# The last output stores of a linear-attention and MLP block: one block half stored by SyncE alone, ScalarE's last stores ordered behind two of SyncE's

## The chip, the cores and the metric

The kernel runs on one core of a Trainium2 chip. The metric is the device time of one execution in microseconds: the median of the runs, 405.24 us for the kernel before. A core has TensorE (PE in the profile), VectorE (DVE), ScalarE (ACT), GpSimd (POOL) and SyncE (SP). SP, ACT and POOL can each issue DMAs, and those of one issuer wait in its own queue; 16 DMA engines move the data.

## The reference

```python
xn = _layernorm(x)                                   # x: 2048 tokens x 512
qkv = xn @ wqkv                                      # 32 heads of 16
pq, pk = phi(q), phi(k)                              # phi(t) = where(t>0, t+1, exp(t)) + 1e-6
kv = einsum("bhsd,bhse->bhde", pk, v);  z = sum_s pk
o = (pq @ kv) / (pq . z + 1e-6)
h = xn @ w1 + b1;  h = relu(h) ** 2                  # 1376 hidden units
return x + o @ wo + (h @ w2 + b2)
```

The output is 2048 x 512 in float32. Only its last stores are touched by the change.

## The kernel before

Tokens are worked on in four blocks of 512. A first part normalises all of them, forms the keys' sums and prepares the weights; then a loop `for n in range(2)` produces the output, two blocks per turn: `t1, t2 = NB - 1 - 2 * n, NB - 2 - 2 * n`. Products of 2x2 blocks are made with Strassen-like combinations (seven products instead of eight), every float32 operand being split into a high and a low part (`split`: ACT rounds the high part, DVE subtracts to get the low one, both in a tile `s`), and three matmul passes are made of the two. At the end of the second turn (n = 1, blocks t1 = 1 and t2 = 0) the partial sums are added up by phases: `phase_jobs(X, 6)`, `phase_jobs(Y, 3)`, `phase_jobs(X, 7)`. What `at_end(...)` names runs after a phase's last job.

An output block is collected in a tile `res[t]` of 128 partitions x 2 halves x 16 x 64. It starts out as x; `add_turned(res[t], c, src)` transposes a result 32 by 32 on DVE (tile `o`) and adds it in. A half (columns 0 to 255 or 256 to 511 of the output) is complete when two such adds are done. In the profile `res[t1]` is res_3127 and `res[t2]` is res_3212.

`store(r, t, *halves, by, blocks)` (line 1315) writes a half with four DMAs, one for each group g = 0, 32, 64, 96 of 32 partitions, each 128 KB in runs of 64 floats. SP issues them; where `by` names another engine, that one issues the groups 32 and 96 (`g.start % 64`) and SP the groups 0 and 64.

Four block halves are stored at the end of the second turn:

- t2's half 1, after phase 6 (line 1633): SP for g = 0 and 64, ACT for g = 32 and 96;
- t1's half 0 (early ready) and half 1, after phase 3 (line 1635): half 0 by SP, half 1 by SP for g = 0 and 64 and by POOL for g = 32 and 96;
- t2's half 0, after the last phase, in two parts of eight 32-token rows each (`PARTS`, `flush`, line 1640): per part SP stores g = 0 and 64, ACT stores g = 32 and 96, 64 KB each. These eight stores of 64 KB are the last work of the program.

What sets the order: the code only records instructions. `Program.order` plans them with costs per instruction, a queue per engine, and dependencies by region of a tile (a write after a read of the same bytes depends on it; writes to the output tensor are not compared). TensorE's own order is fixed as recorded. The instructions are then emitted in the planned order, line 328, which is why nearly all rows of the profile name that line.

A second thing hangs on the emitted order. Every DMA that SP or ACT issues gets one of eight completion semaphores, DMAHW0 to DMAHW7, in turn, over both engines together; before it is issued, the issuing engine waits until the DMA that had the same semaphore eight places earlier has landed. POOL's DMAs have semaphores of their own.

Of the kernel before, what the change touches and what calls it, by code (L numbers as in the profile page):

```python
# [339 lines left out]
def kernel(  # L340
# [12 lines left out]
    nc = Program(tc.nc)  # L353
# [57 lines left out]
    def w512(name, tag, bufs):  # L411
        return work.tile([P, 512], F32, name=name, tag=tag, bufs=bufs)
# [11 lines left out]
    def four(name, tag, dt=F32, pool=None):  # L424
        return (pool or work).tile([P, TB, 512], dt, name=name, tag=tag)
# [13 lines left out]
    def copy(eng, o, i, bias=0.0):  # L439
        if eng == "act":  # L440
            nc.scalar.activation(o, i, AF.Copy, bias=bias)
        elif bias:
            ENG[eng].tensor_scalar(o, i, bias, None, op0=OP.add)
        else:
            ENG[eng].tensor_copy(o, i)
# [600 lines left out]
    for i0 in range(0, NT, TB):  # L1046
# [4 lines left out]
        else:  # L1051
            o = four(f"xg{i0}", "r0" if i0 + TB == NT else "r3")
            a, o = (t.rearrange("p a (g c) -> p (a g c)", g=NJ) for t in (a, o))
            groups[i0 + TB - 1] = [t.rearrange("p (g n) -> p g n", g=NJ) for t in (a, o)]
            a, o = (t.rearrange("p (g i c) -> p g i c", g=NJ, i=TB) for t in (a, o))
# [240 lines left out]
    def out_blocks(w, t):  # L1296

        rows = w[t * BT:(t + 1) * BT, :].rearrange("(b t) n -> t b n", t=32)
        return [(slice(32 * g, 32 * (g + 1)), h, rows[:, :, 256 * h + 64 * g:256 * h + 64 * (g + 1)])
                for h in range(2) for g in range(NJ)]  # L1300

    def load_res(t, pool, tag):
        r = pool.tile([P, 2, BT // 32, 64], F32, name=f"res{t}", tag=tag)
        for g, h, rows in out_blocks(xf, t):
            nc.sync.dma_start(r[g, h], rows)
        return r

    def add_turned(r, c, src, part=slice(0, BT)):
        blocks = slice(part.start // 32, part.stop // 32)
        o = w512("o", "d", 2)[:, :part.stop - part.start]  # L1310
        nc.vector.transpose(o, src[:, part])
        at = r[:, c // 2, blocks].rearrange("p b (d c) -> p b c d", c=2)[:, :, c % 2]
        nc.vector.tensor_tensor(out=at, in0=o.rearrange("p (b d) -> p b d", d=32), in1=at, op=OP.add)

    def store(r, t, *halves, by=None, blocks=slice(0, BT // 32)):
        for g, h, rows in out_blocks(of, t):
            if h in halves:
                (by or nc.sync if g.start % 64 else nc.sync).dma_start(rows[:, blocks], r[g, h, blocks])
# [10 lines left out]
    for n in range(2):  # L1329
        t1, t2 = NB - 1 - 2 * n, NB - 2 - 2 * n  # L1330
# [87 lines left out]
        for p in range(NK + 1):  # L1418
# [20 lines left out]
            if f_before:  # L1439
# [6 lines left out]
                elif p == NK:  # L1446
                    b = [bank(f"late{k}", loop_tag) for k in range(TB)]
                    X, V, Z, Y = b[1:3], [b[3], b[0]], acc[:2], acc[2:]
# [38 lines left out]
        o, ends, res = {}, {}, {}  # L1487
# [7 lines left out]
        def add_to(o, ps):  # L1495
            for c in range(2):
                nc.vector.tensor_tensor(out=o[c], in0=ps[c], in1=o[c], op=OP.add)

        def turned_to(t, a, src):
            for c in range(2):  # L1500
                add_turned(res[t], a + c, src[c])

        def at_end(f):
            ends.setdefault(len(jobs) - 1, []).append(f)
# [94 lines left out]
        X, Z = acc[:2], acc[2:]  # L1599
        res = {t1: load_res(t1, keep, "B0"), t2: load_res(t2, keep, "A0")}  # L1600
# [12 lines left out]
        def phase_jobs(ps, i, first=False, last=False):  # L1613
            return [strassen(ps, k, i, first and k == pairs_f[0], last and k == pairs_f[-1]) for k in pairs_f]
# [15 lines left out]
        jobs.append((lambda: hz[:, 1], lambda s: second_z(W, range(2, NJ), s, True, True)))  # L1630
        at_end(lambda: add_to(o["m5"], W))
        jobs += phase_jobs(X, 6)
        at_end(lambda: (add_to(o["m5"], X), turned_to(t2, 2, o["m5"]), store(res[t2], t2, 1, by=nc.scalar)))
        jobs += phase_jobs(Y, 3, False, True)
        at_end(lambda: (add_to(o["u2"], Y), turned_to(t1, 2, o["u2"]), store(res[t1], t1, 0), store(res[t1], t1, 1, by=nc.gpsimd)))
        jobs.append((lambda: hz[:, 1], lambda s: second_z(X, range(2), s)))
# [2 lines left out]

        def flush(part):  # L1640
            add_turned(res[t2], 1, ends_in[part.start], part)
            store(res[t2], t2, 0, by=nc.scalar, blocks=slice(part.start // 32, part.stop // 32))

        at_end(lambda: run(lambda: add_turned(res[t2], 0, X[0]), *[lambda part=part: flush(part) for part in PARTS]))

        def prepare_s(job):
# [33 lines left out]
```

## Time and profile before

| what | us |
|---|---|
| median of 3 runs (405.2 to 405.49) | 405.24 |
| the profiled execution's own time | 405.01 |
| its span, first to last instruction | 403.3 |
| PE busy | 395.9 (98%) |
| DVE busy | 345.2 (86%) |
| ACT busy | 273.7 (68%) |
| POOL busy | 52.3 (13%) |
| granted TensorE clock | 0.999 |

How to read it: PE is busy nearly throughout, so little but its own work can move the time while it runs. Behind PE's last matmul only DVE's last adds, the eight last stores and the program's end remain; this tail has to be read from the rows of the last microseconds, since shares of the span do not show it. DMA-issuing instructions are listed as `SPq`, `ACTq` and `POOL` rows: their duration is the time that the issuer spends on the issue, not the transfer's.

### The profile page before, as it was taken

The numbers are of one execution on the slowest core, as the hardware profiler recorded it, in microseconds if no ns is written. First come the engines' busy times: TensorE is split into PE (matmuls) and PEld (weight loads), VectorE is DVE, ScalarE is ACT, GpSimd is POOL, SyncE is SP. The second block draws the span as 40 slices with busy tenths as digits, with TensorE's granted clock in tenths as the row PEclk, the third lists the DMA queues.
The fourth block names the chain that finished last, engine by engine and source line by source line (L and its number), as shares of the span: only waits on it lengthen the run. The fifth ranks groups of instructions, "written<-read, shape, count | busy, mean of one in ns | idle before, by whom it ended". The sixth has DMA issues, their size and how long they took to land.

```text
span 403.3 us, 5554 instructions
## 1 busy us (share of the span) xinstructions
PE 395.9 (98%) x1781; PEld 328.3 (81%) x1781; DVE 345.2 (86%) x556; ACT 273.7 (68%) x467; POOL 52.3 (13%) x68
## 2 busy tenths in 40 slices
PE   8999999999999999999999999999999999999994
PEld 7788888888888888888888888888888888888883
DVE  5898998989578989999998899947999999886784
ACT  5786666765859999879986632476968877455430
POOL 2242422120221121220000000031011100000001
PEclk9999999999999999999999999999999999999999
DMA  7962625712398679698627999988998769999345
GB/s 231 292 189 72 201 61 143 295 52 105 122 320 307 232 254 329 242 351 292 265 90 212 325 251 321 287 239 274 301 301 313 243 200 266 234 273 292 111 132 105
DMA packets 77841, 92.00 MB, mean 228 GB/s; under 512 B 39122, under 2 KB 50386, under 8 KB 77556
## 3 DMA queue, kind: packets, MB, share of 16 engines
q1 hardware_dynamic: 75572, 90.86, 73.6%
q10 hardware_dynamic: 2144, 0.52, 0.6%
q0 software_dynamic: 96, 0.26, 0.3%
q8 instruction: 14, 0.23, 0.2%
q14 instruction: 15, 0.12, 0.1%
HBM read 54.67 MB, written 34.87 MB: 222 GB/s over the span
## 4 chain that ended last, share of the span: by engine, by line
PE 96%; DVE 2%; DMA 1%; issue 0%
PE ps L328 54%; PE acc L328 42%; DMA x<-in_A_x_dram 1%; DVE res L328 0%; DVE o L328 0%; DVE st L328 0%; DVE xp L328 0%; DVE y L328 0%; DVE mv L328 0%
## 5 line engine op out<-in xcount | busy, mean ns | idle before, releaser
L328 PE MATMUL ps<-s,ops 128*128 128x512 f32 x417 | 97.9, 389 | 0.0
L328 PEld LDWEIGHTS ps<-s,ops 128*128 128x128 f32 x417 | 78.3, 188 | 16.2
L328 PE MATMUL acc<-s,ops 128*128 128x512 f32 (+1 forms) x246 | 56.6, 381 | 0.0
L328 PEld LDWEIGHTS acc<-s,ops 128*128 128x128 f32 x246 | 45.1, 188 | 8.9
L328 ACT ACTIVATE s<-rr 128x512 fp32r<-128x512 f32 x56 | 35.0, 629 | 19.5 <-DVE s L328 11.0
L328 PE MATMUL acc<-pk,tok 128*128 128x512 f32 x192 | 47.1, 394 | 0.0
L328 DVE TENSOR_TENSOR s<-rr,s 128x512 fp32r<-128x512 f32 x56 | 38.1, 688 | 9.4 <-ACT s L328 7.8
L328 PEld LDWEIGHTS acc<-pk,tok 128*128 128x128 f32 x192 | 35.4, 188 | 7.9 <-DVE pk L328 0.6
L328 PE MATMUL ps<-T,ops 128*128 128x512 f32 x168 | 41.3, 390 | 0.0
L328 PE MATMUL acc<-T,ops 128*128 128x512 f32 x168 | 41.2, 389 | 0.0
L328 PEld LDWEIGHTS acc<-T,ops 128*128 128x128 f32 x168 | 31.5, 188 | 6.6
L328 PEld LDWEIGHTS ps<-T,ops 128*128 128x128 f32 x168 | 31.5, 188 | 6.5
L328 POOL TENSOR_TENSOR tok<-xp,tok 128x512 fp32r<-128x512 f32 x16 | 21.8, 1364 | 43.7 <-ACT tok L328 24.4
L328 POOL TENSOR_TENSOR ops<-s,ops 128x512 fp32r<-128x512 f32 x12 | 15.5, 1296 | 75.0 <-ACT ops L328 60.3
L328 POOL TENSOR_TENSOR made<-t,made 128x512 fp32r<-128x512 f32 x6 | 8.5, 1419 | 125.1 <-ACT made L328 125.1
L328 ACT ACTIVATE rr<-acc 128x512 f32<-128x512 f32 x23 | 13.6, 591 | 15.8 <-PE acc L328 15.7
L328 PE MATMUL ps<-xs0h,ops 128*128 128x512 f32 x72 | 23.6, 389 | 0.0
L328 DVE STREAM_TRANSPOSE d<-d 128x1024 f32<-128x1024 f32 x16 | 19.8, 1235 | 0.1
L328 DVE TENSOR_TENSOR rr<-acc,rr 128x512 f32<-128x512 f32 x21 | 14.4, 687 | 5.9 <-PE acc L328 5.3
L328 ACT ACTIVATE k<-ps 128x512 f32<-128x512 f32 x16 | 9.5, 596 | 13.6 <-PE ps L328 13.5
L328 PE MATMUL acc<-xs0h,ops 128*128 128x512 f32 x56 | 18.4, 389 | 0.0
L328 ACT ACTIVATE rr<-rr,odds 128x512 f32<-128x512 f32 x15 | 10.9, 724 | 10.3 <-DVE rr L328 10.1
(173 smaller groups left out, 782.8 us busy)
## 6 DMA issues: line engine op xcount, KB each, us to landing
wd<-ops SPq DMA_DIRECT2D x35, 512.0 KB, 4.3
ops<-wd SPq DMA_DIRECT2D x56, 256.0 KB, 4.6
ops<-wd SPq DMA_DIRECT2D x27, 512.0 KB, 6.9
wd<-ops SPq DMA_DIRECT2D x19, 256.0 KB, 3.8
res<-in_A_x_dram SPq DMA_DIRECT2D x32, 128.0 KB, 6.1
out_dram<-res SPq DMA_DIRECT2D x24, 128.0 KB, 4.3
wd<-made SPq DMA_DIRECT2D x6, 512.0 KB, 6.2
x<-in_A_x_dram SPq DMA_DIRECT2D x5, 512.0 KB, 6.1
```

Source lines behind the costliest of these rows:

```text
L328: getattr(getattr(self.nc, t.engine), t.name)(*map(real, t.args), **{k: real(a) for k, a in t.kw.items()})
```

## The change

Two edits. The store of t2's half 1 loses its `by=nc.scalar`, so that SP issues all four groups. And in `flush`, for the first part, two columns of `res[t1]` are copied onto themselves by ACT: 32 partitions x 1 element, in half 1, for g = 0 and g = 64. Since SP's two stores of that half read these bytes, the plan must put each copy behind the store that reads it, and the copy waits for the store to land.

```diff
-        at_end(lambda: (add_to(o["m5"], X), turned_to(t2, 2, o["m5"]), store(res[t2], t2, 1, by=nc.scalar)))
+        at_end(lambda: (add_to(o["m5"], X), turned_to(t2, 2, o["m5"]), store(res[t2], t2, 1)))
...
         def flush(part):
             add_turned(res[t2], 1, ends_in[part.start], part)
+            if not part.start:
+                for g in (0, 64):
+                    at = res[t1][g:g + 32, 1, 0, :1]
+                    copy("act", at, at)
             store(res[t2], t2, 0, by=nc.scalar, blocks=slice(part.start // 32, part.stop // 32))
```

SP's queue before, from its last loads (`ops<-wd`) to the program's end; the semaphores that a row waits for stand in brackets (DVE_49 is DVE's count of finished instructions):

```order
L328 DMA ops<-wd_5_91 128x512 [waits DMAHW0_49,PE_49]
L328 DMA ops<-wd_6_92 128x512 [waits DMAHW1_49]
L328 DMA ops<-wd_4_90 128x512 [waits DMAHW2_49,PE_49]
L328 DMA out_dram<-res_3212 32x16x64 [waits DMAHW3_49,DVE_49]
L328 DMA out_dram<-res_3212 32x16x64 [waits DMAHW4_49]
L328 DMA out_dram<-res_3127 32x16x64 [waits DMAHW6_49,DVE_49]
L328 DMA out_dram<-res_3127 32x16x64 [waits DMAHW1_49]
L328 DMA out_dram<-res_3212 32x8x64 [waits DMAHW3_49,DVE_49]
L328 DMA out_dram<-res_3212 32x8x64 [waits DMAHW4_49]
L328 DMA out_dram<-res_3212 32x8x64 [waits DMAHW5_49,DVE_49]
L328 DMA out_dram<-res_3212 32x8x64 [waits DMAHW6_49]
```

SP's queue in the changed kernel, over the same place:

```order
L328 DMA ops<-wd_5_91 128x512 [waits DMAHW6_49,PE_49]
L328 DMA ops<-wd_6_92 128x512 [waits DMAHW7_49]
L328 DMA ops<-wd_4_90 128x512 [waits DMAHW0_49,PE_49]
L328 DMA out_dram<-res_3212 32x16x64 [waits DMAHW1_49,DVE_49]
L328 DMA out_dram<-res_3212 32x16x64 [waits DMAHW2_49]
L328 DMA out_dram<-res_3212 32x16x64 [waits DMAHW3_49]
L328 DMA out_dram<-res_3212 32x16x64 [waits DMAHW4_49]
L328 DMA out_dram<-res_3127 32x16x64 [waits DMAHW5_49,DVE_49]
L328 DMA out_dram<-res_3127 32x16x64 [waits DMAHW6_49]
L328 DMA out_dram<-res_3212 32x8x64 [waits DMAHW0_49,DVE_49]
L328 DMA out_dram<-res_3212 32x8x64 [waits DMAHW1_49]
L328 DMA out_dram<-res_3212 32x8x64 [waits DMAHW3_49,DVE_49]
```

One more store like the last row's, waiting for DMAHW5_49 alone, ends the queue. Two stores more stand ahead of those of res_3127, and the turns of the semaphores have moved. Before, the load `ops<-wd_5_91` waits for DMAHW0, whose holder was ACT's first store of t2's half 1; the last row but one (DMAHW5) waits for ACT's first 64 KB store, and the last (DMAHW6) for SP's first store of res_3127. In the changed kernel the holders that the last four SP rows wait for are a load (DMAHW0), SP's own stores of t2's half 1 (DMAHW1, DMAHW3), and SP's first store of res_3127 (DMAHW5): none is one of the eight last stores.

ACT's queue before, from its last `s` parts on:

```order
L328 ACTIVATE s<-rr_3_2750 128x512 [waits DVE_49,PE_49]
L328 DMA out_dram<-res_3212 32x16x64 [waits DMAHW0_49,DVE_49]
L328 ACTIVATE s<-rr_4_2861 128x512 [waits PE_49,Activation_49]
L328 DMA out_dram<-res_3212 32x16x64 [waits DMAHW5_49,DMAHW3_49]
L328 ACTIVATE s<-rr_5_2966 128x512 [waits PE_49,Activation_49]
...
L328 ACTIVATE s<-rr_3096 128x512 [waits DVE_49,PE_49]
L328 DMA out_dram<-res_3212 32x8x64 [waits DMAHW5_49,DMAHW2_49,DVE_49]
L328 DMA out_dram<-res_3212 32x8x64 [waits DMAHW7_49]
L328 DMA out_dram<-res_3212 32x8x64 [waits DMAHW0_49,DVE_49]
L328 DMA out_dram<-res_3212 32x8x64 [waits DMAHW2_49]
```

ACT's queue in the changed kernel:

```order
L328 ACTIVATE s<-rr_3_2750 128x512 [waits DVE_49,PE_49]
L328 ACTIVATE s<-rr_4_2861 128x512 [waits DVE_49,PE_49]
L328 ACTIVATE s<-rr_5_2966 128x512 [waits DVE_49,PE_49]
...
L328 ACTIVATE s<-rr_3096 128x512 [waits DVE_49,PE_49]
L328 ACTIVATE res_3127<-res_3127 32x1 [waits DMAHW6_49,DMAHW5_49,DVE_49]
L328 DMA out_dram<-res_3212 32x8x64 [waits DMAHW7_49,DMAHW2_49,DVE_49]
L328 ACTIVATE res_3127<-res_3127 32x1 [waits DMAHW6_49,DMAHW3_49]
L328 DMA out_dram<-res_3212 32x8x64 [waits DMAHW3_49,DMAHW2_49]
L328 DMA out_dram<-res_3212 32x8x64 [waits DMAHW4_49,DVE_49]
L328 DMA out_dram<-res_3212 32x8x64
```

The two issues among the `s` parts are gone; of the two copies, one stands ahead of the first of the four last issues and one between the first and the second. DMAHW5 and DMAHW6 are held there by SP's two stores of res_3127.

DVE's queue also came out in another order over ten instructions, here before:

```order
L328 TENSOR_TENSOR u_3453<-acc_73,u_3453 128x512
L328 TENSOR_TENSOR s<-rr_5_2966,s 128x512
L328 TENSOR_TENSOR u_3459<-acc_74,u_3459 128x512
L328 TENSOR_TENSOR s<-rr_0_2461,s 128x512
L328 STREAM_TRANSPOSE o<-u_3453 128x512
L328 TENSOR_TENSOR s<-rr_1_2591,s 128x512
L328 TENSOR_TENSOR res_3127<-o,res_3127 128x512
L328 STREAM_TRANSPOSE o<-u_3459 128x512
L328 TENSOR_TENSOR s<-rr_3096,s 128x512
L328 TENSOR_TENSOR res_3127<-o,res_3127 128x512
```

and in the changed kernel:

```order
L328 TENSOR_TENSOR u_3453<-acc_73,u_3453 128x512
L328 TENSOR_TENSOR u_3459<-acc_74,u_3459 128x512
L328 STREAM_TRANSPOSE o<-u_3453 128x512
L328 TENSOR_TENSOR s<-rr_5_2966,s 128x512
L328 TENSOR_TENSOR res_3127<-o,res_3127 128x512
L328 STREAM_TRANSPOSE o<-u_3459 128x512
L328 TENSOR_TENSOR s<-rr_0_2461,s 128x512
L328 TENSOR_TENSOR res_3127<-o,res_3127 128x512
L328 TENSOR_TENSOR s<-rr_1_2591,s 128x512
L328 TENSOR_TENSOR s<-rr_3096,s 128x512
```

The second add into res_3127, for which SP's and POOL's stores of t1's half 1 wait, moves from the tenth place to the eighth; the low parts of the last two operands move behind it.

## The prediction

> **What bounds the kernel now.** I read the page first: PE is busy for 98% of the span, and the chain of waits is PE nearly throughout. So I went to the end of that chain, in order of time (start, duration, what):
>
> ```profile
> PE 96%; DVE 2%; DMA 1%; issue 0%
> 377.05 9.52 PE acc L328 x42
> 386.57 8.85 PE ps L328 x39
> ...
> 398.10 0.43 DVE res L328
> ```
>
> PE works without a gap through the place that the change touches, from 377.05 on. The chain ends with DVE's last add at 398.53 (398.10 + 0.43), but the span ends at 403.3: the 4.8 us between are stores, which the chain does not follow. So I read the timeline of the issuers there (start, duration, issuer):
>
> ```profile
> 396.83 0.66 POOL L328 DMA_DIRECT2D out_dram<-res  x1 [2.58 <-issue]
> 397.73 0.32 SPq L328 DMA_DIRECT2D out_dram<-res  x1
> 397.74 2.01 ACTq L328 DMA_DIRECT2D out_dram<-res  x4
> 398.72 0.43 ACTq L328 DMA_DIRECT2D out_dram<-res  x1
> 399.19 0.56 ACTq L328 DMA_DIRECT2D out_dram<-res  x1
> 400.18 0.32 SPq L328 DMA_DIRECT2D out_dram<-res  x1
> 400.54 0.45 SPq L328 DMA_DIRECT2D out_dram<-res  x1
> ```
>
> ACT has issued its four stores by 399.75, the third at 398.72, just after DVE's last add. SP, which needs the same add, starts its third only at 400.18 and its fourth at 400.54. The waits of SP's queue behind 398, and a little earlier (us in total, times, longest), say why:
>
> ```profile
> SPq L328 <- DMA out_dram<-res: 1.6, 1, 1.6
> SPq L328 <- DMA out_dram<-res: 12.4, 1, 12.4
> ```
>
> The first row is SP's third last store, 1.6 us behind the landing of another store. By the order above it waits for DMAHW5, which ACT's first 64 KB store holds. The second is the wait between 374 and 387 of SP's last three loads, behind ACT's first store of t2's half 1 (DMAHW0). It costs nothing now, since PE has no gap there.
>
> How long a store takes from issue to landing, by the DMA view of single moments (ACT's first at 397.74; ACT's last at 399.19; SP's at 400.18 and 400.54):
>
> ```profile
> out_dram<-res ACTq DMA_DIRECT2D x1, 64.0 KB, 2.4
> ...
> out_dram<-res ACTq DMA_DIRECT2D x1, 64.0 KB, 2.1
> ...
> out_dram<-res SPq DMA_DIRECT2D x1, 64.0 KB, 1.7
> ...
> out_dram<-res SPq DMA_DIRECT2D x1, 64.0 KB, 1.8
> ```
>
> 397.74 + 2.4 is 400.14, where SP resumes: the releaser is confirmed. The end is 400.54 + 1.8 = 402.34, and the span ends 0.96 behind that, the program's end. The profiled execution took 405.01, 1.71 more than its span and 0.23 below the median of 405.24. I make the sum against the landing at 402.34 and take the difference from the median.
>
> **The change, part by part.** *ACT's two stores of t2's half 1 go to SP.* On ACT this removes two issues of 0.3 to 0.4 us among `s` parts that wait for PE or DVE anyway: nothing gained. On SP four issues, of up to 0.45 each by the rows above, follow the add into res_3212 that ends at 384.49 (383.80 + 0.69, row below), where SP now stands in its 12.4 us wait; they are done by about 386.3, and no load is behind them. The loads ahead of them no longer wait for ACT's store and go out about 10 us sooner. That gains nothing either, as PE has no gap, and the buffers they fill are released by PE as before. What covers this is SP's idle time up to its stores of res_3127.
>
> *DVE's order.* Rows of before (the add into res_3212 just named, the start of the ten instructions, ACT's last `s` part, the tenth, the stores behind it):
>
> ```profile
> 383.80 0.69 DVE L328 TENSOR_TENSOR res<-o,res 128x512 f32<-128x512 f32 x1
> ...
> 386.58 0.68 DVE L328 TENSOR_TENSOR u<-acc,u 128x512 f32<-128x512 f32 x1
> ...
> 390.68 0.63 ACT L328 ACTIVATE s<-rr 128x512 fp32r<-128x512 f32 x1 [0.67 <-PE ps L328]
> ...
> 392.46 0.68 DVE L328 TENSOR_TENSOR res<-o,res 128x512 f32<-128x512 f32 x1
> 393.16 0.85 SPq L328 DMA_DIRECT2D out_dram<-res  x2
> 393.40 0.72 DVE L328 STREAM_TRANSPOSE o<-ps 128x512 f32<-128x512 f32 x1 [0.27 <-PE ps L328]
> 393.46 0.80 POOL L328 DMA_DIRECT2D out_dram<-res  x1 [79.10 <-DVE res L328]
> ```
>
> Ten instructions start over 5.88 us, 0.65 apart. Two places up, the second add into res_3127 ends 1.3 us sooner, near 391.8. SP's stores of t1's half 1 and POOL's follow it: SP at 391.9 instead of 393.16, POOL's first at 392.1, its second, which came 3.37 us behind the first, at 395.5 instead of 396.83. The last two low parts of `s` end near 392.9 instead of 392.54; PE begins the job that reads them when the bank is finished that DVE picks up at 393.40. So 0.5 us of cover remains, and if it went, PE would be late by what is over.
>
> *POOL's second store is out of the way.* It took 2.7 us to land (first row; behind it SP's two stores of res_3127, for the next part):
>
> ```profile
> out_dram<-res POOLq DMA_DIRECT2D x1, 128.0 KB, 2.7
> ...
> out_dram<-res SPq DMA_DIRECT2D x1, 128.0 KB, 2.2
> ...
> out_dram<-res SPq DMA_DIRECT2D x1, 128.0 KB, 2.5
> ```
>
> Before it is in flight until 399.5, beside the first of the last stores; now until 398.2, when those have only been issued.
>
> *The two copies.* Each waits for one of SP's stores of res_3127 to land: issued at 391.9 and 392.3, landing 2.2 to 2.5 later, by 394.8. ACT has been free since 391.3 and is next needed at 397.74, so 2.9 us hide the wait. Behind the waiting copy stand ACT's four last stores; the end of the program waits for them. The second copy finds its store landed and costs ACT's issue path only its own dispatch. The trace has no such copy. The nearest rows (an ACT instruction of one element a row with its mean, and a DMA issue that directly follows an ACT instruction):
>
> ```profile
> L328 ACT ACTIVATE y<-y 128x1 f32<-128x1 f32 x5 | 1.0, 203 | 0.2
> 385.30 0.63 ACT L328 ACTIVATE s<-rr 128x512 fp32r<-128x512 f32 x1 [0.79 <-DVE s L328]
> 385.38 0.32 ACTq L328 DMA_DIRECT2D out_dram<-res  x1
> ```
>
> The issue starts 0.08 behind the start of an instruction that it doesn't depend on, so the copy costs 0.08 at least and 0.08 + 0.20 = 0.28 if the issue waits for its end. I take 0.1, as the store doesn't read what is copied. ACT's last issue moves from 399.19 to 399.3. It cannot become a gain, since nothing ahead of it is removed.
>
> *SP's last two stores lose their wait.* The third goes out when DVE's add is done, as ACT's did: near 398.7 instead of 400.18, the fourth near 399.1 instead of 400.54. With 1.7 to 1.8 us to land they would be done by 400.9. So ACT's last store is late next: 399.3 + 2.1 = 401.4. But eight stores are now in flight where there were six, so the transfer itself must be bounded. The windows (times, four engines and POOL, clock, DMA share, GB/s):
>
> ```profile
> 393.90:395.60 1.70, 1.70 (x11) 1.47 (x10) 1.07 (x3) 0.00 (x0) 0.35 (x1) 1.00 0.84 169
> 398.60:399.10 0.50, 0.00 (x0) 0.00 (x0) 0.00 (x0) 0.00 (x0) 0.00 (x0) 1.00 0.60 119
> 398.60:400.85 2.25, 0.00 (x0) 0.00 (x0) 0.00 (x0) 0.00 (x0) 0.00 (x0) 1.00 0.88 179
> 399.60:400.10 0.50, 0.00 (x0) 0.00 (x0) 0.00 (x0) 0.00 (x0) 0.00 (x0) 1.00 1.04 215
> 400.10:400.60 0.50, 0.00 (x0) 0.00 (x0) 0.00 (x0) 0.00 (x0) 0.00 (x0) 1.00 1.09 233
> 402.00:403.30 1.30, 0.00 (x0) 0.00 (x0) 0.00 (x0) 0.00 (x0) 0.00 (x0) 0.57 0.02 6
> ```
>
> Eight times 64 KB is 524 KB, from 398.6 on. At 119 GB/s for half a microsecond (60 KB) and then between the best two rows, 224, the last byte moves at 398.6 + 0.5 + 2.07 = 401.17; at 179 throughout, at 401.53. The last packets of before moved at 402.0, 0.34 ahead of the landing, so the end is 401.5 or 401.9. Against 401.4 from the issues I take 401.5, the fast drain: with eight stores offered early the slow ramp should be short, and POOL's bytes are gone.
>
> **The sum.** Landing 402.34 to 401.5: 0.84 us less. Copy (0.1) and drain are in it, the rest is hidden. 405.01 - 0.84 = 404.17 for this execution, 405.24 - 0.84 = 404.4 for the median. Its own range runs from 404.1 (last ACT store lands within 1.8: 401.1) to 404.7 (slower rate after the ramp: 401.8). 0.2% is 0.81 us, about what a measurement of this kernel can tell from no change, so the forecast lies almost on that line.
>
> **The rivals.** *The engines drain no faster (0.17).* The end is now a transfer: 2.25 us of the last 3.4 run at a DMA share of 0.88 already. At the 169 GB/s of SP's two stores alone, 524 KB take 3.10 us: last byte at 401.7, landing 402.04, 0.3 gained, 404.9. For it: the rate with two queues over 2.25 us, 179, is hardly above one queue's 169. Against: 215 and 233 in the two best half microseconds. The Trainium skill, "DMA: Bandwidth & Descriptors", section "Issuing engines are not separate DMA queues", says that DMAs of all issuers run on the same 16 engines and that issuing from several only saves issue time; the trace agrees so far (169 against 179).
>
> *The wait only moves (0.04).* SP's last stores would wait for another late landing, 405.2. Against: the holders that they now wait for have landed by about 394.5.
>
> *The copies hold ACT up: slower (0.07).* The wait of the first copy replaces the one removed. If SP's stores of res_3127 land late, all of ACT's last issues are late. The point from which it decides: the copies' stores must land behind 397.7 to cost anything, and about 1.7 us behind that to cost 0.81 on the whole. The longest landings in the trace:
>
> ```profile
> ops<-wdz SPq DMA_DIRECT2D x5, 512.0 KB, 8.3
> DMA to landing us min/median/max: 1.7/3.6/5.3
> ```
>
> The second is of all output stores: 392.3 + 5.3 = 397.6 is still in time. With the 8.3 of the largest loads, landing at 400.6, ACT's last store lands about 2.9 later than 401.5, at 404.4: 407.3. Nothing that large is in flight there, hence the small chance.
>
> *More than forecast (0.10).* ACT's stores also land faster without POOL's, by 401.1: 404.0.
>
> **How the numbers follow.** The forecast itself has 0.62; of it 0.43 lies beyond 0.81 us, as ACT's issues alone would end at 401.4, and 0.19 within. Faster: 0.43 + 0.10 = 0.53. Same: 0.19 + 0.17 + 0.04 = 0.40. Slower: 0.07. The range runs from 403.9, a little beyond the fast case, to 405.1, beyond the slow drain; it leaves out the moved wait and the slower rival.
>
> **What would show it.** Right: SP's third and fourth of the last stores start near 398.7 and 399.1, the 1.6 us wait of its queue is gone, the copies run near 394 with ACT's next issue still at 397.74, POOL's second issue is near 395.5, the last landing is near 401.5, and PE shows no new gap. Wrong: ACT's first last issue later than 397.8, a rate below 180 GB/s from 398.6 on, SP still waiting for a store behind 398, or PE waiting for an `s` near 394.

## The result, and the profile after

The changed kernel takes 404.6 us (median of 22 runs, 404.36 to 405.61), the kernel before 405.23 us (22 runs, 404.94 to 406.29): 0.63 us less. The ratio is 0.9984, with a 95% interval of 0.9977 to 0.999. The profiled execution took 404.68 us with a span of 403.0.

In this execution everything runs 0.2 us later than in the profiled one of before by the time the tail begins, so times are best taken from the end of DVE's last add, here 398.33 + 0.42 = 398.75. The timeline of the changed kernel's tail (start, duration, issuer): DVE's last add, SP's four last stores, ACT's four with the copies, POOL's two.

```profile
398.33 0.42 DVE L328 TENSOR_TENSOR res<-o,res 128x256 f32<-128x256 f32 x1
397.97 0.32 SPq L328 DMA_DIRECT2D out_dram<-res  x1
398.33 0.45 SPq L328 DMA_DIRECT2D out_dram<-res  x1
398.90 0.40 SPq L328 DMA_DIRECT2D out_dram<-res  x1
399.33 0.47 SPq L328 DMA_DIRECT2D out_dram<-res  x1
...
393.92 0.20 ACT L328 ACTIVATE res<-res 32x1 f32<-32x1 f32 x1 [2.37 <-DMA out_dram<-res]
397.97 0.39 ACTq L328 DMA_DIRECT2D out_dram<-res  x1
398.46 0.20 ACT L328 ACTIVATE res<-res 32x1 f32<-32x1 f32 x1 [4.34 <-DVE o L328]
398.55 0.32 ACTq L328 DMA_DIRECT2D out_dram<-res  x1
398.96 0.41 ACTq L328 DMA_DIRECT2D out_dram<-res  x1
399.40 0.49 ACTq L328 DMA_DIRECT2D out_dram<-res  x1
...
391.94 0.80 POOL L328 DMA_DIRECT2D out_dram<-res  x1 [77.36 <-DVE res L328]
395.27 0.66 POOL L328 DMA_DIRECT2D out_dram<-res  x1 [2.54 <-issue]
```

SP's third and fourth stores now go out at 398.90 and 399.33, beside ACT's, and not at 400.18 and 400.54. The first copy waits for the landing of SP's store of res_3127 and is through at 394.1, 3.8 us ahead of ACT's next issue. POOL's stores start 1.5 us sooner. The waits of SP's queue behind 398 show the same: no wait of a line of the kernel's body for a store is left, only those of the program's end (L1679).

```profile
SPq L328 <- DVE res L328: 5.4, 1, 5.4
SPq L1679 <- DMA out_dram<-res: 1.8, 4, 0.6
SPq L1679 <- PEq L1679: 0.6, 2, 0.5
```

What ends last now, by the DMA view at 399.5 (SP's and ACT's fourth store, us from issue to landing), and the windows of the drain, the stretch in which the engines move the eight stores (times, engines, clock, DMA share, GB/s):

```profile
out_dram<-res SPq DMA_DIRECT2D x1, 64.0 KB, 2.5
out_dram<-res ACTq DMA_DIRECT2D x1, 64.0 KB, 2.6
```

```profile
398.83:399.33 0.50, 0.00 (x0) 0.00 (x0) 0.00 (x0) 0.00 (x0) 0.00 (x0) 1.00 0.87 183
399.33:399.83 0.50, 0.00 (x0) 0.00 (x0) 0.00 (x0) 0.00 (x0) 0.00 (x0) 1.00 0.98 191
399.83:400.33 0.50, 0.00 (x0) 0.00 (x0) 0.00 (x0) 0.00 (x0) 0.00 (x0) 0.76 0.87 154
400.33:400.83 0.50, 0.00 (x0) 0.00 (x0) 0.00 (x0) 0.00 (x0) 0.00 (x0) 0.50 1.06 214
400.83:401.33 0.50, 0.00 (x0) 0.00 (x0) 0.00 (x0) 0.00 (x0) 0.00 (x0) 0.50 1.09 229
398.83:401.65 2.82, 0.00 (x0) 0.00 (x0) 0.00 (x0) 0.00 (x0) 0.00 (x0) 0.72 0.92 185
```

ACT's last store is issued as long behind DVE's last add as before (0.65 against 0.66 us) but takes 2.6 us to land, not 2.1: the last landing is at 399.40 + 2.6 = 402.0. From DVE's last add to the last landing it is 3.25 us, before 3.8 (398.53 to 402.34). These 0.56 us are the gain of the two profiled executions; the interval of the runs, 0.4 to 0.9 us, holds them. Over the 2.82 us of the drain the DMA share is 0.92. Single rows go above 1, so the times that the profile gives to packets overlap, and a share is no exact measure of how full an engine is.

### The profile page after: what moved, and what is told of

Same layout as the page of the kernel before. It is cut to its first block, busy times and chain, and to the rows that moved or that the text cites. A ratio compares the mean times of both kernels' runs of the same rounds, so it can differ in the third digit from the quotient of the medians.

```text
span 403.0 us, 5557 instructions
## 1 busy us (share of the span) xinstructions
PE 395.1 (98%) x1781; PEld 327.4 (81%) x1781; DVE 344.9 (86%) x556; ACT 274.1 (68%) x469; POOL 52.3 (13%) x68
## 4 chain that ended last, share of the span: by engine, by line
PE 96%; DVE 2%; DMA 1%; issue 0%
PE ps L328 54%; PE acc L328 42%; DMA x<-in_A_x_dram 1%; DVE res L328 0%; DVE o L328 0%; DVE st L328 0%; DVE xp L328 0%; DVE y L328 0%; DVE mv L328 0%
```

## The experiments

Theory A: the gain is the removed wait of SP for a store that was itself among the last eight. Rival B: it comes from moving the four stores to SP, by what ACT need no longer issue and the loads that go out sooner. Rival C: it comes from POOL's stores, which DVE's new order lets start sooner. And for what is left of the tail: theory D, the bytes set the end; theory E, issue and landing latency do.

For each run this table has the median, that of the kernel before beside it, and the tail of the profiled execution: from the end of DVE's last add to the last landing. Landings are given to 0.1 us, so a tail is good to about 0.05.

| kernel | median us | before us | ratio, interval | tail us |
|---|---|---|---|---|
| before | | 405.23 | | 3.8 |
| changed | 404.6 | 405.23 | 0.9984, 0.9977 to 0.999 | 3.25 |
| first edit alone | 405.65 | 405.16 | 1.0002, 0.9991 to 1.0012 | 4.2 |
| copies alone | 404.58 | 405.16 | 0.9987, 0.9978 to 0.9996 | 3.25 |
| before, no POOL stores | 404.98 | 405.16 | 0.9992, 0.9983 to 1.0 | 3.65 |
| changed, no POOL stores | 404.64 | 405.23 | 0.9985, 0.9977 to 0.9994 | 3.25 |
| changed, half the bytes | 403.76 | 405.16 | 0.9965, 0.9952 to 0.9978 | 2.3 |
| changed, half runs | 403.83 | 405.23 | 0.9962, 0.995 to 0.9974 | 2.45 |

**The first edit alone** (on the kernel before):

```diff
-        at_end(lambda: (add_to(o["m5"], X), turned_to(t2, 2, o["m5"]), store(res[t2], t2, 1, by=nc.scalar)))
+        at_end(lambda: (add_to(o["m5"], X), turned_to(t2, 2, o["m5"]), store(res[t2], t2, 1)))
```

> The first edit alone: SP issues all four stores of t2's half 1, and there are no copies. In the built program SP's four last stores now wait for semaphores held by SP's or ACT's own last stores: the first for ACT's first 64 KB store, the third for ACT's second, the fourth for ACT's third. Theory A (what counts is SP's wait for the landing of a store that was itself among the last eight): the first of SP's last four starts only when ACT's first has landed, 2.2 to 2.4 us behind its issue at about 397.7, so near 400.1; four issues of 0.3 to 0.45 us end near 401.6, the last landing comes near 403.1, 0.8 us later than before: 406.0 us. Theory B (moving the four stores to SP is itself the gain, because ACT has less to issue and the loads go out sooner): the 0.65 us of the whole change, 404.6 us.

Measured: 405.65 us against 405.16. The medians are 0.49 us apart, but the kernel before has single runs up to 406.67 in this series, and the interval of the ratio reaches from a gain of 0.1% to a loss of 0.1%, so the runs alone settle no sign. Theory B's 0.65 us less (a ratio of 0.9984) lies outside it, and the profile shows what happens instead. DVE's last add, SP's wait behind 394, ACT's first store of the last eight with SP's first, which waits for it, and SP's last:

```profile
398.37 0.43 DVE L328 TENSOR_TENSOR res<-o,res 128x256 f32<-128x256 f32 x1
...
SPq L328 <- DMA out_dram<-res: 5.5, 1, 5.5
...
398.01 0.38 ACTq L328 DMA_DIRECT2D out_dram<-res  x1
out_dram<-res ACTq DMA_DIRECT2D x1, 64.0 KB, 1.8
...
399.83 0.32 SPq L328 DMA_DIRECT2D out_dram<-res  x1
...
401.20 0.46 SPq L328 DMA_DIRECT2D out_dram<-res  x1
out_dram<-res SPq DMA_DIRECT2D x1, 64.0 KB, 1.8
```

SP stands for 5.5 us until ACT's first store has landed, at 398.01 + 1.8, and issues all its four stores behind that; the last lands at 403.0, 4.2 us behind DVE's last add. That is theory A's mechanism, with a smaller price than expected (0.4 us on the tail instead of 0.8), as the store that is waited for lands in 1.8 us when SP's are not in flight beside it, against 2.4 before. Moving the stores to SP gains nothing by itself. DVE's order and POOL's times are those of the kernel before here (POOL's second store starts at 397.00).

**The copies alone** (on the kernel before):

```diff
             add_turned(res[t2], 1, ends_in[part.start], part)
+            if not part.start:
+                for g in (0, 64):
+                    at = res[t1][g:g + 32, 1, 0, :1]
+                    copy("act", at, at)
             store(res[t2], t2, 0, by=nc.scalar, blocks=slice(part.start // 32, part.stop // 32))
```

> The second edit alone: ACT still issues two of the four stores of t2's half 1, and the two copies stand ahead of ACT's last stores. In the built program none of the eight last stores waits for another of them, DVE's order is that of the changed kernel, and SP's three last loads still wait for ACT's store near 386. Theory A: the whole gain, 404.6 us, 0.65 less than before, with SP's third and fourth last stores near 398.9 and 399.3. Theory B: no gain, 405.2 us.

Measured: 404.58 us, as the changed kernel. DVE's last add, the long wait of SP's queue from 374 on, its third and fourth last stores and ACT's fourth:

```profile
398.15 0.43 DVE L328 TENSOR_TENSOR res<-o,res 128x256 f32<-128x256 f32 x1
...
SPq L328 <- DMA out_dram<-res: 11.7, 1, 11.7
...
398.69 0.41 SPq L328 DMA_DIRECT2D out_dram<-res  x1
399.15 0.46 SPq L328 DMA_DIRECT2D out_dram<-res  x1
399.21 0.49 ACTq L328 DMA_DIRECT2D out_dram<-res  x1
out_dram<-res ACTq DMA_DIRECT2D x1, 64.0 KB, 2.6
```

The long wait of SP's loads for ACT's store is still there, 11.7 us, and costs nothing; the short one at the end is gone, and the whole gain is there. So theory B falls: the copies do it, and beside them the first edit makes no difference that these runs can tell. DVE's new order comes with the copies too, so this run doesn't tell theory A from rival C.

**POOL's stores left out**, of the kernel before and of the changed one (`by is nc.gpsimd` marks t1's half 1):

```diff
-                (by or nc.sync if g.start % 64 else nc.sync).dma_start(rows[:, blocks], r[g, h, blocks])
+                if by is not nc.gpsimd or g.start % 64 == 0:
+                    (by or nc.sync if g.start % 64 else nc.sync).dma_start(rows[:, blocks], r[g, h, blocks])
```

> The kernel before without POOL's two stores of t1's half 1, so a quarter of that block's half is not written; all orders and waits else as before. It tells what POOL's store in flight until 399.5 costs the last stores. Theory A: SP's third last store still waits for ACT's first to land; that landing takes 2.2 us instead of 2.4, so the end comes 0.1 to 0.3 us sooner: 405.0 us. Rival C (the changed kernel gains because POOL's store comes sooner): nearly the whole gain, 404.6 to 404.7 us.

> The changed kernel without POOL's two stores of t1's half 1, so these are not written. Beside the kernel before without them (0.18 us faster by the medians than with them) it splits the gain. Theory A (the removed wait is the gain, POOL's store only adds to it by being out of the way): POOL's last store lands at 397.7 in the changed kernel, ahead of the last stores' first packets, so leaving it out changes next to nothing: from DVE's last add to the last landing 3.2 us instead of 3.26, 404.5 to 404.6 us. Rival C (POOL's traffic still weighs on the tail): another 0.2 us or more, 404.4 us or less.

Measured: before without them 404.98 us, 0.18 less than with them, where the interval of the ratio just reaches 1; changed without them 404.64 us, no less than with them. In the kernel before without POOL's stores (DVE's last add; SP's waits behind 399; the landing of ACT's first last store; SP's last store and its landing):

```profile
399.25 0.43 DVE L328 TENSOR_TENSOR res<-o,res 128x256 f32<-128x256 f32 x1
...
SPq L328 <- DMA out_dram<-res: 1.4, 1, 1.4
...
out_dram<-res ACTq DMA_DIRECT2D x1, 64.0 KB, 2.2
...
401.51 0.45 SPq L328 DMA_DIRECT2D out_dram<-res  x1
out_dram<-res SPq DMA_DIRECT2D x1, 64.0 KB, 1.8
```

This profiled execution took 405.95 us, about 1 us over the median, and all of that lies ahead of the tail; its tail is read from the end of its own last add, 399.68. The landing that SP waits for takes 2.2 us instead of 2.4, so SP's wait is 1.4 instead of 1.6 and the tail 0.15 to 0.2 shorter. The changed kernel without POOL's stores (DVE's last add, the second copy, ACT's last store and its landing):

```profile
398.32 0.42 DVE L328 TENSOR_TENSOR res<-o,res 128x256 f32<-128x256 f32 x1
...
394.31 0.20 ACT L328 ACTIVATE res<-res 32x1 f32<-32x1 f32 x1 [0.28 <-DMA out_dram<-res]
...
399.39 0.49 ACTq L328 DMA_DIRECT2D out_dram<-res  x1
out_dram<-res ACTq DMA_DIRECT2D x1, 64.0 KB, 2.6
```

In the changed kernel nothing is left for POOL's stores to delay, since they have landed at 395.27 + 2.4 = 397.7. Leaving them out also moves the second copy ahead of ACT's first issue, and the tail stays 3.25 us all the same. Without POOL's stores the change shortens the tail by 3.65 - 3.25 = 0.4 us (404.98 - 404.64 = 0.34 by the medians), with them by 0.55. So 0.35 to 0.4 us are the removed wait, which theory A names, and 0.15 to 0.2 are POOL's store being out of the way; the second part is too small for the runs to tell from nothing, and rests on the profiles. Rival C holds for that smaller part. That DVE's order is what moved POOL's store was not tried by itself; in the profiles the two go together: the second add into res_3127 starts at 392.46 and 392.67 in the kernel before and with the first edit alone, at 390.82 and 390.93 with the copies alone and in the changed kernel, and POOL's first store follows its start by 1.0 us in all four.

**Half the bytes** (the changed kernel, each of the last eight stores cut to four of its eight blocks):

```diff
-            store(res[t2], t2, 0, by=nc.scalar, blocks=slice(part.start // 32, part.stop // 32))
+            store(res[t2], t2, 0, by=nc.scalar, blocks=slice(part.start // 32, part.start // 32 + 4))
```

> The changed kernel with each of the eight last stores cut to its first four blocks of 32 tokens, 32 KB instead of 64 KB; the other half of t2's half 0 is not written. The number of issues and their order on each engine are kept, one semaphore's turn apart. It tells whether the end is now set by the bytes or by the issues. Theory D (the 16 DMA engines drain 524 KB from 398.9 on without a pause, about 190 GB/s, and this sets the end): half the bytes need 1.4 us, the end is then set by ACT's last issue near 399.4 and a landing of 1.7 to 2.0 us, 401.1 to 401.4 instead of 402.0: 403.7 to 404.0 us. Theory E (issue and landing latency set the end whatever the bytes): as the changed kernel, 404.6 us.

Measured: 403.76 us. DVE's last add, ACT's last store, its landing, and the window of the drain with its packets:

```profile
398.08 0.43 DVE L328 TENSOR_TENSOR res<-o,res 128x256 f32<-128x256 f32 x1
...
399.10 0.46 ACTq L328 DMA_DIRECT2D out_dram<-res  x1
out_dram<-res ACTq DMA_DIRECT2D x1, 32.0 KB, 1.7
...
398.55:400.45 1.90, 0.00 (x0) 0.00 (x0) 0.00 (x0) 0.00 (x0) 0.00 (x0) 1.00 0.66 137
DMA packets 1141, 0.26 MB, mean 137 GB/s; under 512 B 1141, under 2 KB 1141, under 8 KB 1141
```

ACT's last issue stands 0.59 us behind DVE's last add (0.65 in the changed kernel), the landing takes 1.7 us instead of 2.6, the DMA share falls to 0.66. Theory D holds: once SP's wait is gone, the drain of the eight stores sets the end, and halving it takes 0.95 us off the tail. What is left is then set by ACT's last issue and its landing.

**Half runs** (the changed kernel, each of the last eight stores with as many runs, of 128 bytes instead of 256):

```diff
-                (by or nc.sync if g.start % 64 else nc.sync).dma_start(rows[:, blocks], r[g, h, blocks])
+                (by or nc.sync if g.start % 64 else nc.sync).dma_start(*(v[:, blocks, :32] if blocks.stop - blocks.start == 8 else v for v in (rows, r[g, h])))
```

> The changed kernel with each of the eight last stores writing 32 of its 64 columns: as many runs as in the changed kernel, each of 128 bytes instead of 256; the other columns of t2's half 0 are not written. It tells apart what of the drain counts. If the number of runs sets it (2048 packets, about 790 in a microsecond), the end is that of the changed kernel, 404.6 us. If the bytes set it, the end is that of half the bytes, 403.8 us.

Measured: 403.83 us, as with half the bytes. DVE's last add, ACT's last store, its landing, the drain's window and its packets; and the packets of the changed kernel's drain (398.83 to 401.65):

```profile
398.61 0.42 DVE L328 TENSOR_TENSOR res<-o,res 128x256 f32<-128x256 f32 x1
...
399.67 0.48 ACTq L328 DMA_DIRECT2D out_dram<-res  x1
out_dram<-res ACTq DMA_DIRECT2D x1, 32.0 KB, 1.8
...
399.05:401.10 2.05, 0.00 (x0) 0.00 (x0) 0.00 (x0) 0.00 (x0) 0.00 (x0) 1.00 0.80 128
DMA packets 2176, 0.26 MB, mean 128 GB/s; under 512 B 2176, under 2 KB 2176, under 8 KB 2176
```

```profile
DMA packets 2162, 0.52 MB, mean 185 GB/s; under 512 B 2162, under 2 KB 2162, under 8 KB 2162
```

The number of packets does not set the end: as many of them, 2176 against 2162 in the two windows, are through in 2.05 us instead of 2.82, with the engines at a share of 0.80. Half as many bytes in as many packets gain what half as many packets gain. At shares of 0.66 and 0.80 neither drain fills the engines any more, and both kernels end with ACT's last issue and a landing of 1.7 or 1.8 us, so these two runs don't weigh bytes against packets any finer than that.

## Why the prediction was right, and where its size was off

**The wait.** Right: SP's 1.6 us wait for ACT's first store was named, it went, and it is the larger part of the gain (0.35 to 0.4 us), as the pair of kernels without POOL's stores shows. That the first edit and the earlier loads gain nothing was right too, as the two single edits show.

**DVE's order and POOL.** Right in direction, larger in size: the second add came far enough forward for POOL to start 1.5 us sooner (1.3 forecast, and this execution runs 0.2 us late besides), POOL's second store landed at 397.7 (398.2 forecast), and PE has no new gap.

**The copies.** The first ran at 393.92 (near 394 forecast) under the cover named. The second lies between ACT's first and second issue: from 398.36 to 398.55, 0.19 us, where before it was 0.04 (398.11 to 398.15). Its cost is 0.15 us, between the bounds of 0.08 and 0.28 and near the 0.1 taken. But it did not move ACT's last issue, since the third issue waits for DVE's last add anyway and stands 0.21 us behind it (0.19 before). In the changed kernel without POOL's stores the second copy runs at 394.31, well ahead, and ACT's last issue is again 0.65 us behind the add. The 0.1 that the prediction put on ACT's last issue was not paid.

**The drain** is the term that was mis-sized. The prediction took 119 GB/s for half a microsecond and then 224, the mean of the two best rows, so the last byte 2.57 us behind the first. It took 2.82 us at a mean of 185: the first half microsecond was faster than taken (183), the next two slower (191 and 154), and rates of 214 and 229 came only behind 400.3. So the best half microseconds of before were peaks and no rate for the whole; why the rate swings so is open. The mean over the 2.25 us of before, 179, would have come nearer: at 179 throughout the prediction's own last byte comes 2.93 us behind the first, and with it the gain would have been near 0.5 us; 0.56 is what the tail shows, 0.63 what the runs show, and 0.84 was forecast. The other bound of the end, ACT's last issue and a landing of 2.1 us, failed by the same step: with eight stores in flight the landing took 2.6 us, and with half the bytes 1.7.

So the slow end of the prediction's own range is what came: it gave a landing at 401.8, and 402.0 less the 0.23 us by which this execution runs late is 401.77. Its chances leaned the other way, with 0.53 on more than 0.81 us and 0.40 on less. Its reason to take the fast drain, that eight stores offered early make the slow ramp short, was half right: the ramp was short, but the rate behind it was not that of the peaks.

**Smaller slips of the prediction** that the forecast does not hang on: a landing at 401.1 gives 404.0 by its own working, not the 404.1 that its range begins with. The 169 GB/s of SP's two stores alone holds 0.03 MB of POOL's first store; SP's own 0.26 MB in that window make about 154. And the 8.3 us of the largest loads is the median of five, not the longest.

**The rivals.** That the engines drain no faster came about half true: the mean rate with eight stores is 185 GB/s against 179 with six, but not 169, and the wait's removal still paid. The Trainium skill, "DMA: Bandwidth & Descriptors", section "Issuing engines are not separate DMA queues", says that all issuers share the same 16 engines; the trace agrees (185 against 179). The moved wait and the copies that hold ACT up did not come. The first edit alone shows what the moved wait would have been: SP's first store then waits instead of its third.

The rows of the queues above also show how the turns come about. Before, ACT's four last stores take the turns 5, 7, 0 and 2, around SP's two stores of res_3127 (6 and 1) and ahead of all of SP's last four (3 to 6); so SP's third finds ACT's first as the holder eight places earlier. In the changed kernel ACT's four come behind both stores of res_3127 (5 and 6) and alternate with SP's last four, and the holders that SP meets are old ones. That the copies do this by making ACT's last stores follow SP's stores of res_3127 is read from these rows; no other way to the same turns was run.

## What to carry to other kernels

When an issuer waits for a DMA that has nothing to do with its data, look for a completion semaphore that is used in turn: the holder eight places earlier is what it waits for, and an ordering that puts the stores of an earlier tile ahead makes the holder one that has long landed. Price the end that is uncovered by the mean rate of a drain over its whole length, not by its best half microsecond: here 185 GB/s was measured where 179 was the mean before and 224 the peak. And try the parts of such a change apart: here one edit alone lengthens the tail of its profile, and the other alone gives all of the gain.

## What the runs showed that was not expected

As many runs of half the length gained as much as half as many runs of full length. From the rows, a packet of 256 bytes took 16 x 0.92 x 2.82 / 2162 = 19 ns of an engine, one of 128 bytes 16 x 0.80 x 2.05 / 2176 = 12 ns, a ratio of 0.63. With half the bytes, where the engines are less full, a packet of 256 bytes took 16 x 0.66 x 1.90 / 1141 = 18 ns, and the ratio is 0.69. So a packet's time here is neither fixed nor in proportion to its bytes. The Trainium skill, "DMA: Bandwidth & Descriptors", section "Why small descriptors are slow (HBM only)", gives a fixed overhead of about 3 cycles a packet beside one for each 32 bytes, 11 cycles for 256 bytes; by it, as an estimate, 128 bytes would take 7, a ratio of 0.64. The trace is near that with 0.63 and 0.69; that this overhead is the cause was not tried.

The landing of a 64 KB store also depends on what flies beside it more than expected. For ACT's first store it is 1.8 us with SP waiting (POOL's second store is in flight there too), 2.2 with SP's beside it and POOL's left out, and 2.4 with both.
